# Attention with two dense stages on one core: the first keys on one queue, and other loads of the attention stage at other steps

## The chip, the cores and the metric

The kernel runs on one core of one Trainium2 chip. The metric is the device time of one execution in microseconds; the time before is the median of three executions, 612.26 us (610.55 to 615.47).

## The reference

The reference has three stages on one token matrix: an attention in which the 12 heads are mixed before and after the softmax, and two dense blocks.

```python
scores = scale * np.matmul(q, k.transpose(0, 1, 3, 2))       # batch 2, 12 heads, 448 x 448, head size 64
scores = np.einsum('bhij,hg->bgij', scores, w_pre)
scores = scores - np.max(scores, axis=-1, keepdims=True)
attn = np.exp(scores)
attn = attn / (np.sum(attn, axis=-1, keepdims=True) + 1e-09)
attn = np.einsum('bhij,hg->bgij', attn, w_post)
x = np.matmul(attn, v)                                       # then 896 tokens x 768
h = x @ moe_w_in;  x = np.where(h > 0, h, np.exp(np.minimum(h, 0)) - 1) @ moe_w_out
h = x @ moe2_w_in; x = (h / (1 + np.exp(-h))) @ moe2_w_out   # 768 -> 2048 -> 768, both times
```

All of it is in 32-bit floats.

## The kernel before, in words

The schedule is written out by hand: each engine executes its instructions in the order in which the program emits them, and each of the two load queues that are used (SP's and ACT's) issues its transfers in that order too.

**Start.** The queries come in seven tiles of 128 rows (`qT[T]`, all heads, 6 pairs of heads each), the keys as one tile per pair of heads (`kT[p]`, both batches side by side). Ahead of the loop the program issues, pair by pair, the keys of batch 0 (line 291), with the first query tile in two parts on ACT's queue (line 293); then the mixing weights `kpre` on ACT's queue, the second query tile, `kps`, a first part of v of batch 0 (heads 0 to 2, all partitions) and the third query tile on SP's queue. TensorE executes warm-up matmuls on zeros (line 306), then the scores of the first query tile, pair of heads by pair (`qk_pair`, line 148), in order of the pairs; ACT and DVE scale each pair's scores into `s` (lines 155 and 157).

**Blocks.** Mixing the heads needs the heads on the partitions. So 10 query rows of a tile make a block: a move from on-chip memory to on-chip memory (`move`, line 166) puts 10 rows of all 12 heads into the buffer `blk`, of which there are three, each for two blocks. `relayout(s)` issues the moves of step s, two to four of them, on SP's queue.

**Loop.** There are 45 steps. In step s TensorE executes `premix(s)` (line 196, reads `blk`), then attention times v for some heads of an older tile (`av_pair`, line 263, at the steps of `AV_AT`), then one pair of scores of a later query tile, then `postmix(s - 1)` (line 235). DVE takes the maximum, ACT the exponential, POOL scales the small weights `krn`, and ACT and DVE copy the result into `a`. At the end of step s the program issues `relayout(s + 2)` and then what the table `D_AT` holds for step s: query tiles, keys of batch 1 and parts of v, in this order, all on SP's queue. SP waits only where a buffer isn't free or a tile isn't there yet, so it is ahead of TensorE by some steps' worth of issues.

**Tables that bear on the change.** The keys of batch 1 are issued in steps 7 to 12, one pair in each. The fourth query tile (T = 3) is issued in step 7 and read in steps 10 to 15, one pair in each. v of batch 0 is loaded in parts of three heads (g) and half the partitions (u). `AV_AT` reads them so: step 8 reads heads 0 to 3, step 10 reads heads 4 to 7, step 12 reads heads 8 to 11; each matmul reads all partitions, so both halves u. In step 12 the matmuls on heads 8 and 9 alternate, so the second one already reads the part of heads 9 to 11 (g = 3). Before the change the parts g = 1 to 3 were issued in steps 2 to 7, one in each.

**Afterwards** come the two dense blocks, with each weight matrix split into a high and a low part (lines 497 to 549) and matmuls on both (lines 543, 805 and 1065). They are the larger part of the span.

Of the kernel before, what the change touches and what calls it, by code (L numbers as in the profile page):

```python
# [22 lines left out]
NP = H // 2  # L23
# [53 lines left out]
def attn_moe_moe(ctx: ExitStack, tc: tile.TileContext, q, k, v, w_pre, w_post, w1i, w1o, w2i, w2o, out):  # L77
    nc = tc.nc
# [34 lines left out]
    def load_q(T, eng=None, parts=(slice(0, NP),)):  # L113
        if T not in qT:
            qT[T] = wp.tile([P, NP, 2 * P], F32, name=f"qt{T}", tag="qT", bufs=3).rearrange("p a b -> p (a b)")[:, :NP * P].rearrange("p (a b) -> p a b", a=NP)
        for p in parts:
            (eng or nc.sync).dma_start(qT[T][:, p], q[T, :, p])

    def load_k(b, p, eng=None):
        if b == 0:  # L120
            kT[p] = kp.tile([P, 2, S], F32, name=f"kt{p}", tag=f"kT{p}")
        (eng or nc.sync).dma_start(kT[p][:, b], k[b, p])

    def load_v(b, u, g):

        h = slice(3 * g, 3 * g + 3)
        o = slice(0, P) if u is None else slice(HS * u, HS * u + HS)
        nc.sync.dma_start(vall[b][o, h].rearrange("p h r d -> p (h r d)"), v[b, o, 768 * g:768 * g + 768])
# [159 lines left out]
    nc.vector.memset(wz, 0.0)  # L288
    nc.vector.memset(pad[0:1], 0.0)
    for p in range(NP):  # L290
        load_k(0, p, (nc.sync, nc.scalar)[p in (2, 4)])
        if p < 2:
            load_q(0, nc.scalar, (slice(0, 2), slice(2, NP))[p:p + 1])
    nc.scalar.dma_start(kpre, w_pre)
# [25 lines left out]
    QK_AT, X_AT, D_AT = {}, {}, {}  # L320

    def at(d, step, f):
        d.setdefault(int(step), []).append(f)
# [2 lines left out]
        for p in range(LEAD if T == 1 else 0, NP):  # L326
            at(QK_AT, n0 + p, lambda T=T, p=p: qk_pair(T, p))
    for T in range(3, NQ):
        at(D_AT, (7, 13, 17, 24)[T - 3], lambda T=T: load_q(T))
    AV_AT = (8, 10, 12, 14, 16, 18, 20, 22, 23, 24, 26, 28, 30, 32, 34, 36, 38, 40, 42, 43, 44)  # L330
    for T in range(NT_ - 1):
        for p in range(NP):
# [3 lines left out]
    for g in range(4):  # L336
        for u in range(2):
            for b in range(B):
                if b == 1 or g > 0:
                    at(D_AT, 2 * g + u + (21 if b else 0), lambda b=b, u=u, g=g: load_v(b, u, g))  # L340

    def run(d, s):
        for f in d.get(s, []):
# [641 lines left out]
    x = [t[:, i] for t in rr for i in range(3)] + [xq[1, 5]] + [xq[1, p] for p in range(5)]  # L985
    xt[1] = {}
    for t, n_ in zip(x, "B11_0 B11_1 B11_2 T1_0 T1_1 T1_2 B21_0 B21_1 B22_0 T2_0 T2_1 B22_1 T3_0 T3_1 T4_0 T4_1 B21_2 T2_2 T3_2 T4_2 B22_2".split()):
        a, i = n_.split("_")
# [19 lines left out]
    for f in range(KF):  # L1008
        x = f + 2 if f < KS else f - KS
        raw[1, f] = rt[x // 3][:, x % 3] if x < 9 else rk[x - 9]  # L1010
    hb[1] = rk[3:]
    x = [ge[u][:, i] for u in range(2) for i in range(3)] + [gs[:, i] for i in range(6)]
# [106 lines left out]
    while n < NCH:  # L1119
# [5 lines left out]
        i = n - O2  # L1125
# [90 lines left out]
```

## Time and profile before

| | us |
|---|---|
| median of three runs | 612.26 |
| the three runs | 610.55, 612.26, 615.47 |
| the profiled execution | 608.93 |
| its span, first to last instruction | 607.1 |
| TensorE busy in it | 591.5 (97%) |
| VectorE, ScalarE, GpSimd busy | 451.0, 372.2, 62.7 |

The profile is of one execution, and its times are counted from the first instruction. An engine's busy time is the time in which it executes; a wait is time in which it is idle, and the profile says which event ended it. "SPq" and "ACTq" are the queues' issues of transfers: the time of such a row is that of issuing, not of moving the bytes. A transfer's landing is seen where somebody waits for it. The 45 steps of the attention stage lie in about the first quarter of the span.

### The profile page before, as it was taken

Reading aid. Unit: us, or ns where it says so; the run is one execution under the profiler, and the core shown is the slowest. Engines: PE = TensorE matmul, PEld = TensorE weight load, DVE = VectorE, ACT = ScalarE, POOL = GpSimd, SP = SyncE. Lnnn points to the kernel's source line nnn. Section 1 sums busy time; section 2 is a strip of 40 time slices with the busy share of each in tenths; the row PEclk is TensorE's granted clock in tenths of the full one; section 3 lists DMA queues with packets and bytes.
Section 4 is the critical chain, followed back from the end, with each engine's and each line's share of the span. In section 5 each row is a group of like instructions: output and inputs, shape, how many; then the busy total and the mean of one; then the engine's idle time right before and its main releaser. Section 6 shows DMA issues by size and latency. Waiting matters only on the chain.

```text
span 607.1 us, 14991 instructions
## 1 busy us (share of the span) xinstructions
PE 591.5 (97%) x6139; PEld 506.3 (83%) x6139; DVE 451.0 (74%) x756; ACT 372.2 (61%) x686; POOL 62.7 (10%) x117
## 2 busy tenths in 40 slices
PE   7899999998899999999999999999999999999997
PEld 2456766566699899999999999999999999999996
DVE  4777776888747999886776675599888888966642
ACT  4667776787838966758783553377676666533311
POOL 1222222247360000000000000000000000000000
PEclk9999999999999999999999999999999999999999
DMA  6577557755403243432434323434333323453601
GB/s 229 197 219 234 165 144 213 208 183 191 158 2 116 93 157 104 131 108 83 130 105 148 96 87 115 145 105 156 119 141 105 120 87 107 138 168 111 224 2 60
DMA packets 37682, 82.04 MB, mean 135 GB/s; under 512 B 4205, under 2 KB 18285, under 8 KB 37613
## 3 DMA queue, kind: packets, MB, share of 16 engines
q1 hardware_dynamic: 36749, 80.08, 41.7%
q8 instruction: 48, 0.79, 0.5%
q10 hardware_dynamic: 864, 1.00, 0.5%
q14 instruction: 21, 0.17, 0.1%
HBM read 59.05 MB, written 2.75 MB: 102 GB/s over the span
## 4 chain that ended last, share of the span: by engine, by line
PE 81%; DVE 6%; ACT 6%; DMA 5%; issue 1%; ACTq 0%; POOL 0%; DVEq 0%; SPq 0%; POOLq 0%
PE po L543 31%; PE b L805 28%; DMA blk<-s 4%; ACT pe L210 4%; PE av L263 4%; PE q L1065 4%; PE pre L196 3%; PE ph L529 3%; PE post L235 3%; PE pq L148 2%; PE po L1065 2%; DVE nmx L202 2%; DVE a L134 2%; PE post L529 1%; DMA kt<-in_k_dram 1%
## 5 line engine op out<-in xcount | busy, mean ns | idle before, releaser
L805 PE MATMUL b<-x,we 128*128 128x448 f32 x360 | 93.8, 363 | 0.0
L210 ACT ACTIVATE pe<-pre,nmx 124x448 f32<-124x448 f32 x90 | 56.3, 630 | 36.8 <-DVE nmx L202 35.9
L805 PEld LDWEIGHTS b<-x,we 128*128 128x128 f32 x360 | 67.5, 188 | 4.7 <-DVE we L549 0.2
L805 PE MATMUL b<-rr,we 128*128 128x448 f32 x288 | 69.5, 362 | 0.0
L757 ACT ACTIVATE wr<-wr 128x768 f32<-128x768 f32 (+1 forms) x61 | 52.9, 867 | 18.2 <-DMA wr<-in_w1o_dram 8.3
L235 PEld LDWEIGHTS post<-krn,pe 60*64 60x64 f32 x2520 | 45.6, 135 | 21.5 <-POOL krn L223 10.2
L543 PE MATMUL po<-ge,we 128*128 128x448 f32 x216 | 60.3, 362 | 0.0
L543 PE MATMUL po<-gs,we 128*128 128x448 f32 x216 | 59.9, 362 | 0.0
L753 DVE SCALAR_TENSOR_TENSOR wc<-wr,wc 128x768 int32<-128x768 int32 (+1 forms) x62 | 56.2, 907 | 3.9 <-ACT wr L757 0.4
L805 PEld LDWEIGHTS b<-rr,we 128*128 128x128 f32 x288 | 54.1, 188 | 3.5
L202 DVE TENSOR_REDUCE nmx<-pre 124x1 f32<-124x448 f32 x90 | 51.6, 615 | 4.2 <-PE pre L196 3.8
L196 PE MATMUL pre<-blk,kpre 64*64 64x448 f32 x360 | 48.7, 543 | 2.6 <-DMA blk<-s 2.0
L263 PEld LDWEIGHTS av<-a,v 128*64 128x64 f32 x768 | 36.9, 137 | 16.9 <-ACT pe L210 6.3
L543 PE MATMUL po<-x,we 128*128 128x448 f32 x192 | 50.1, 362 | 0.0
L235 PE MATMUL post<-krn,pe 60*64 60x60 f32 x2520 | 46.4, 219 | 3.6 <-POOL krn L223 2.8
L500 DVE TENSOR_TENSOR we<-wc,we 128x640 fp32r<-128x640 f32 (+1 forms) x31 | 26.7, 863 | 30.8 <-ACT we L491 30.8
L223 POOL TENSOR_SCALAR krn<-kps,sum 124x60 f32<-124x60 f32 x90 | 37.6, 432 | 113.3 <-DVE sum L219 96.4
L543 PE MATMUL po<-ta,we 128*128 128x448 f32 x168 | 44.8, 362 | 0.0
L148 PE MATMUL pq<-kt,qt 64*64 64x448 f32 x336 | 41.4, 561 | 2.5 <-ACT s L155 1.2
L263 PE MATMUL av<-a,v 128*64 128x120 f32 (+1 forms) x768 | 41.7, 262 | 1.6 <-ACT a L132 1.6
L543 PEld LDWEIGHTS po<-gs,we 128*128 128x128 f32 x216 | 40.6, 188 | 2.6
L543 PEld LDWEIGHTS po<-ge,we 128*128 128x128 f32 x216 | 40.6, 188 | 2.6
(155 smaller groups left out, 1079.4 us busy)
## 6 DMA issues: line engine op xcount, KB each, us to landing
blk<-s SPq DMA_DIRECT2D x77, 210.0 KB
wr<-in_w1i_dram SPq DMA_DIRECT2D x32, 384.0 KB
wr<-in_w2i_dram SPq DMA_DIRECT2D x32, 384.0 KB
wr<-in_w1o_dram SPq DMA_DIRECT2D x24, 384.0 KB
wr<-in_w2o_dram SPq DMA_DIRECT2D x24, 384.0 KB
wr<-in_w1o_dram SPq DMA_DIRECT2D x12, 256.0 KB
wr<-in_w2o_dram SPq DMA_DIRECT2D x12, 256.0 KB
v<-in_v_dram SPq DMA_DIRECT2D x14, 192.0 KB
```

The costliest lines, as they stand in the source:

```text
L148: nc.tensor.matmul(pq[e][HS * c:HS * c + HS], qT[T][half, p, HS * c:HS * c + HS], kT[p][half, bs[c % len(bs)]], start=True, stop=True, til ...
L196: nc.tensor.matmul(pre[s][r][HS * c:HS * c + HS], kpre[o], blkb[o, s % NBUF, c], start=True, stop=True, tile_position=(HS * r, HS * c))
L202: nc.vector.tensor_reduce(nmx[s][:n, r:r + 1], pre[s][r][:n], axis=AX.X, op=ALU.max, negate=True)
L210: nc.scalar.activation(t[:n], pre[s][r][:n], AF.Exp, bias=nmx[s][:n, r:r + 1], scale=1.0, accum_out=sums[s][:n, r:r + 1])
L223: nc.gpsimd.tensor_scalar(t[:n], kps[:n], z[:n, r:r + 1], None, op0=ALU.mult)
L235: nc.tensor.matmul(w[c][HS * u:HS * u + HS, r, j * BW:(j + 1) * BW], pexp[s][r][o, m * HS:(m + 1) * HS], kr[s][r][o].rearrange("p h i -> p ...
L263: nc.tensor.matmul(avt[T][e * D:(e + 1) * D, p % 2, :m], vall[b][:NV, h, j], amap[T][:NV, j * H + h, :m], start=j == 0, stop=j == 3, tile_ ...
L543: nc.tensor.matmul(po, wt[:, kk * P:(kk + 1) * P], g_op(moe, k0 + kk, hf, gi), start=(k0 == 0 and n_ == 0), stop=(k0 + kn == (KF, KS)[moe] ...
L753: nc.vector.scalar_tensor_tensor(cc, r[:, :, 1], 3, cc, op0=ALU.logical_shift_left, op1=ALU.bitwise_or)
L757: nc.scalar.activation(hf, hf, AF.Prelu, scale=2.0 ** -112, alpha=2.0 ** 32)
L805: nc.tensor.matmul(o, wt[:, u * KH + i * P:u * KH + (i + 1) * P], X[x, i][:, xi], start=start and n_ == 0, stop=n_ == 8, skip_group_check= ...
L1065: nc.tensor.matmul(o, wt[:, u * KH + i * P:u * KH + (i + 1) * P], t[i][:, xi] if x == "B22" else t[:, i, xi], start=start and n_ == 0, sto ...
```

## The change

Three things are changed. All six keys of batch 0 are issued on SP's queue, in the order of the pairs; before, pairs 2 and 4 were on ACT's queue. The fourth query tile is loaded in three parts of two pairs, in steps 7, 8 and 10, not whole in step 7. The parts of v of batch 0 (g, u) = (1,0), (1,1), (2,0), (2,1), (3,0), (3,1) are issued in steps 2, 4, 5, 6, 9, 11, not in steps 2 to 7. The parts of v of batch 1 stay in steps 21 to 28.

```diff
     for p in range(NP):
-        load_k(0, p, (nc.sync, nc.scalar)[p in (2, 4)])
+        load_k(0, p)
         if p < 2:
             load_q(0, nc.scalar, (slice(0, 2), slice(2, NP))[p:p + 1])
...
     for T in range(3, NQ):
-        at(D_AT, (7, 13, 17, 24)[T - 3], lambda T=T: load_q(T))
+        for i, s in enumerate(((7, 8, 10), (13,), (17,), (24,))[T - 3]):
+            at(D_AT, s, lambda T=T, x=slice(2 * i, 2 * i + 2) if T == 3 else slice(0, NP): load_q(T, None, (x,)))
...
                 if b == 1 or g > 0:
-                    at(D_AT, 2 * g + u + (21 if b else 0), lambda b=b, u=u, g=g: load_v(b, u, g))
+                    at(D_AT, 2 * g + u + 21 if b else (2, 4, 5, 6, 9, 11)[2 * g + u - 2], lambda b=b, u=u, g=g: load_v(b, u, g))
```

## Rows read from the trace of the kernel before

**Rows 1.** The page, its chain that ended last, by engine.

```profile
PE 81%; DVE 6%; ACT 6%; DMA 5%; issue 1%; ACTq 0%; POOL 0%; DVEq 0%; SPq 0%; POOLq 0%
```

**Rows 2.** Stretches: bounds, length, busy by engine (instructions), clock, DMA share, GB/s.

```profile
2.00:4.00 2.00, 1.98 (x4) 0.67 (x2) 0.09 (x1) 0.00 (x0) 1.05 (x1) 1.00 0.89 315
4.00:6.00 2.00, 1.98 (x12) 0.74 (x16) 0.11 (x1) 1.62 (x3) 0.00 (x0) 1.00 1.05 349
6.00:8.00 2.00, 0.84 (x12) 0.24 (x8) 1.14 (x2) 0.94 (x2) 0.00 (x0) 1.00 1.01 379
...
36.00:42.00 6.00, 5.67 (x110) 3.34 (x112) 4.42 (x11) 4.24 (x12) 1.67 (x4) 1.00 0.86 227
...
48.00:54.00 6.00, 6.00 (x176) 4.23 (x174) 4.41 (x9) 3.80 (x10) 0.84 (x2) 1.00 0.76 227
```

**Rows 3.** Timeline of the start: start, duration, engine, line, operation, [idle before].

```profile
0.73 0.89 ACTq L117 DMA_DIRECT2D qt<-in_q_dram  x2
0.73 1.81 SPq L122 DMA_DIRECT2D kt<-in_k_dram  x4
...
1.38 2.60 PE L306 MATMUL warm<-wz 128*128 128x448 f32 x4 [1.38 <-DVE align L289]
...
1.65 0.93 ACTq L122 DMA_DIRECT2D kt<-in_k_dram  x2
...
4.02 2.54 PE L148 MATMUL pq<-kt,qt 64*64 64x448 f32 x16
...
7.72 5.73 PE L148 MATMUL pq<-kt,qt 64*64 64x448 f32 x56 [1.16 <-DMA kt<-in_k_dram]
```

**Rows 4.** Chain of waits up to 70 us: start, duration, what.

```profile
1.65 5.93 DMA kt<-in_k_dram
...
11.75 2.83 DMA blk<-s
...
33.42 5.59 DMA blk<-s
...
40.53 6.35 DMA blk<-s
```

**Rows 5.** Timeline of SP's queue, steps 7 to 11.

```profile
36.60 1.64 SPq L117 DMA_DIRECT2D qt<-in_q_dram  x1
38.29 0.42 SPq L122 DMA_DIRECT2D kt<-in_k_dram  x1
38.75 0.75 SPq L128 DMA_DIRECT2D v<-in_v_dram  x1
39.61 1.71 SPq L166 DMA_DIRECT2D blk<-s  x2
...
48.79 1.71 SPq L166 DMA_DIRECT2D blk<-s  x2
50.54 0.51 SPq L122 DMA_DIRECT2D kt<-in_k_dram  x1
```

**Rows 6.** Timeline of TensorE, steps 10 to 13.

```profile
45.76 0.97 PE L196 MATMUL pre<-blk,kpre 64*64 64x448 f32 x4
46.92 0.97 PE L196 MATMUL pre<-blk,kpre 64*64 64x448 f32 x4 [0.20 <-DMA blk<-s]
...
53.55 0.94 PE L196 MATMUL pre<-blk,kpre 64*64 64x448 f32 x8
54.42 1.86 PE L263 MATMUL av<-a,v 128*64 128x120 f32 x32
```

**Rows 7.** The page, DMA issues: what, queue, operation, count, KB each.

```profile
v<-in_v_dram SPq DMA_DIRECT2D x14, 192.0 KB
```

**Rows 8.** DMA issues of the whole span, the same columns.

```profile
qt<-in_q_dram SPq DMA_DIRECT2D x6, 384.0 KB
kt<-in_k_dram SPq DMA_DIRECT2D x10, 224.0 KB
```

**Rows 9.** Waits of TensorE, whole span: total us, times, longest us.

```profile
PE pre L196 <- DMA blk<-s: 2.0, 4, 1.3
```

## The prediction

> **What bounds the kernel now.** I read the chain of waits first. 81% of it is TensorE, 5% is transfers [rows 1], and the dense blocks, which the change doesn't touch, hold most of the TensorE part. So only a few microseconds can move. Next I looked in the attention stage for the places where the chain passes through a transfer. Four pieces bear on the change [rows 4]. The first is the keys, 5.93 us from an issue at 1.65 to a landing at 7.58. The second is the first block move, 2.83 us. The last two are moves of steps 6 and 8, 5.59 and 6.35 us. The block moves have the same kind and size, so the reader sees a queue: with little ahead of it a move lands 2.83 us after its issue, and from about 33 us on two to three times as late. The stretches agree, with 0.86 and 0.76 of the transfer engines busy at 227 GB/s in the last two lines of [rows 2]. Third, the timeline of TensorE: the second half of the mixing of step 10 starts at 46.92 after a start of the first at 45.76 [rows 6], when its move has landed at 40.53 + 6.35 = 46.88 [rows 4].
>
> My sum is made against the profiled execution, 608.93 us with a span of 607.1. The median of the runs shown is 612.26, so 3.33 us more; I add the sum to the median.
>
> **First keys.** TensorE finishes the scores of pairs 0 and 1 at 4.02 + 2.54 = 6.56 and starts pair 2 at 7.72; 1.16 us of idle time are put down to keys [rows 3]. These are the keys of pair 2, third on ACT's queue behind two parts of the queries, while SP's queue moves pairs 3 and 5, which are wanted later. The transfer engines are full meanwhile (share 0.89 to 1.05), with 315, 349 and 379 GB/s in three stretches [rows 2], so the bytes ahead decide. In the new order pair 2 needs 384 + 3 x 224 = 1056 KB [rows 8], 1081 thousand bytes. By 4.00 us 630 thousand have moved, and the other 451 take 1.29 us at 349 GB/s: 5.29. Pair 0 gives the lag to the use: its 128 + 224 KB, 360 thousand bytes, are moved by 2 + 360/315 = 3.14, and it starts at 4.02, 0.88 later. So pair 2 is there at 6.17, before TensorE is through with pair 1. The pairs behind need 229 thousand bytes each, 0.6 to 0.66 us at these rates, and are used one per 5.73/7 = 0.82 us [rows 3], so no new wait follows. On SP the two issues that join the queue cost 2 x 0.45 us (1.81 for four [rows 3]); they lie beside the transfers, which are late anyway. The next issue on SP, the second query tile, moves behind them by at most 0.9 us, and its scores come after those of pair 5. Two issues leave ACT's queue, where nothing waits for them. Bounds: between nothing (the slowest transfer engine, not the mean, sets a landing) and 1.16 us. I take a gain of 1.0, nearer to the row of the wait. All of it lies on the path: the scores of pair 5 release the first move at 11.75 [rows 4].
>
> The Trainium skill, in "DMA: Bandwidth & Descriptors", section "Issuing engines are not separate DMA queues", says that transfers issued by different engines run on the same 16 engines and that issuing from several saves issue time alone. By that rule alone the edit would gain nothing and lose up to those 0.9 us, and the sum below would be 3.2 in place of 1.3. The rule leaves out that of the bytes on their way some are wanted earlier than others.
>
> **Fourth query tile and v.** In step 7 SP issues q (384 KB), keys (224) and v (192) ahead of the moves at 39.61 [rows 5, 7, 8]. After the change it issues 128 + 224 KB there. 448 KB less stand ahead of the moves for step 10, about 459/227 = 2.0 us of transfer, so the 1.16 us between the halves of the mixing in step 10 [rows 6] should go. The parts of the queries in steps 8 and 10 add two issues of about 0.4 us (the keys' 0.42 [rows 5]) on SP, which is ahead of TensorE. Parts one to three are read from steps 10, 12 and 14 on, at least two steps behind their issue; I cost them at nothing, and the cover is those two steps, 7.8 us as from 45.76 to 53.55 [rows 6], against a landing in 5.59 to 6.35.
>
> What is late next is v. From step 7 to step 11 SP issues 384 + 5 x 224 + 192 = 1696 KB before, and 1888 KB after, for the v part of step 3 drops out early, where it disturbed nobody, and two parts come late. So at step 11 the queue isn't shorter but 192 KB longer. The last part, (3,1), is issued at the end of step 11, behind the moves at 48.79 and the keys, which are issued at 50.54 + 0.51 = 51.05 [rows 5]. TensorE starts the attention times v of step 12 at 54.42 [rows 6] and its second matmul needs this part. **The price:** with the landing times of the loaded queue, 5.59 and 6.35, the part lands at 56.6 to 57.4; with that of the empty one, 2.83, at 53.9. The stretch from 48 to 54 moves 227 GB/s, as that from 36 to 42 [rows 2], so the loaded rows are the nearest. Against 54.42 that is 2.2 to 3.0 us late, and nothing in the other bound. I take 2.3, near the low end, since SP reaches the place a little earlier when step 7 gives it less to issue. Behind the waiting matmul stand all later TensorE instructions: the scores, the mixing after the softmax of step 11 and the mixing of step 13, and with them the maxima on DVE and the exponentials on ACT. From 48 to 54 TensorE is busy for 6.00 of 6.00 us [rows 2], so it can't catch up. The 1.16 us of step 10 aren't subtracted from this: TensorE only comes earlier to the place where it waits for the landing, and its idle time there grows to about 3.4 us.
>
> The wait of the moves that land at 39.01 (33.42 + 5.59) stays, since the v parts of steps 4 to 6, which stand around them, stay.
>
> **Sum:** -1.0 + 2.3 = +1.3 us. 608.93 becomes 610.2, the median 613.6.
>
> **Rivals.**
> *The part lands in time.* The queue would have to be drained by step 11; the moves land 2.83 us behind their issue where it is [rows 4], and the bound of 53.9 lies before 54.42. Against it stand the two loaded rows. Then both gains hold: -1.0 - 1.16 = -2.2, a median of 610.1.
>
> *The clock falls in the stall, which makes the kernel slower by more.* The first 16 score matmuls take 2.54 us, 0.159 each, and the later 56 take 5.73, 0.102 each [rows 3]: until then TensorE had executed nothing but the warm-up from 1.38 on, and it runs slower, though the granted clock is given as 1.00 in these stretches [rows 2]. Its longest waits for transfers are 1.3 us [rows 9] and don't show this afterwards (the 56 follow one of 1.16). A stall of 3.4 us is longer than any of these. From that length on, if the clock then falls to the lower of its two levels, 1.2 GHz, the price is between 16 x 0.057 = 0.9 us and half of the 5.2 us from 1.38 to 6.56, that is 2.6; I take 2.0. Sum +3.3, a median of 615.6. "TensorE: Matmul & The Clock Gate" of the Trainium skill, section "HAM oscillation — how this bites in real kernels", describes such a fall in waits for transfers; no row here shows a wait as long as this stall.
>
> *The first keys gain nothing,* as the change in order may not do what it says if the slowest transfer engine is late with pair 2 in any order: and the two issues on SP then cost up to 0.9 us: +2.3 to +3.2, a median of 614.6 to 615.5. For it speaks that shares above 0.89 hide single engines; against it the order of the bytes.
>
> **How the numbers follow.** Chances: the forecast 0.58, the part in time 0.22, the clock 0.13, no gain from the keys 0.07. The likeliest gives 613.6. Its own bounds are -1.16 + 2.2 to +3.0 (a key gain of nothing), so 613.3 to 615.3. The three runs of before lie between -1.7 and +3.2 of their median, so a median of such runs can be off by 1 to 2. The range takes in the rival below with that, 609, and the one above, 617. A change of 1%, 6.1 us, is about what a measurement of this kernel can tell from none. For the faster side all gains that I find make 2.2; for the slower side the highest price is 3.0 + 2.6 = 5.6. So faster 0.02, same 0.94, slower 0.04.
>
> **What would show it.** Right: pair 2 starts without a wait for keys, near 6.6, and the first move is issued near 10.8; the halves of step 10's mixing are no longer apart; in step 12 TensorE idles for some 3 us within the first matmuls on v, put down to the landing of v, and the mixing of step 13 starts 1 to 2 us later than before. Wrong: the matmuls on v in step 12 follow the mixing at once (then it is -2.2), or those behind the stall take twice their time (+3.3). The forecast also fails if a later stage gives the time back, which would show as a shorter span behind the attention stage.

## The result, and the profile after

The changed kernel takes 615.55 us (median of 22 runs), the kernel before in the same runs 611.87 us. The ratio is 1.0076 (95% interval 1.0055 to 1.0097), some 4.6 us of 612. Each ratio in this document comes from the single runs, without the executions in a slower state that some kernels have (up to 627 us), so it isn't the quotient of the two medians, which here differ by 3.7 us. The profiled execution of the changed kernel takes 615.15 us with a span of 613.3, so 6.2 us over that of before.

The chain of waits of the changed kernel, up to 75 us (start, duration, what), answers to [rows 4]:

```profile
3.98 7.41 PE pq L148 x56
11.39 2.83 DMA blk<-s
...
32.25 6.38 DMA blk<-s
...
44.99 1.34 issue
...
51.82 5.68 DMA v<-in_v_dram
...
57.63 2.15 PE av L263 x30
```

The keys are gone from it, and the first block move is issued at 11.39, not 11.75. The move of step 6 is as late as before (32.25 + 6.38 = 38.63, before 39.01). Two new pieces have come: 1.34 us in which TensorE waits for nothing that the profile names ("issue"), and a load of v that lands at 57.50.

TensorE's timeline of the changed kernel (start, duration, line, operation, [idle before]), which answers to [rows 3, 6]:

```profile
3.97 9.12 PE L148 MATMUL pq<-kt,qt 64*64 64x448 f32 x72
...
44.48 0.51 PE L235 MATMUL post<-krn,pe 60*64 60x60 f32 x18
46.33 0.74 PE L235 MATMUL post<-krn,pe 60*64 60x60 f32 x35 [1.34 <-issue]
...
53.54 0.94 PE L196 MATMUL pre<-blk,kpre 64*64 64x448 f32 x8
54.41 0.42 PE L263 MATMUL av<-a,v 128*64 128x120 f32 x2
57.63 2.15 PE L263 MATMUL av<-a,v 128*64 128x120 f32 x30 [2.80 <-DMA v<-in_v_dram]
59.71 1.77 PE L148 MATMUL pq<-kt,qt 64*64 64x448 f32 x8
61.26 1.51 PE L235 MATMUL post<-krn,pe 60*64 60x60 f32 x56
62.60 0.93 PE L196 MATMUL pre<-blk,kpre 64*64 64x448 f32 x8
```

The last of these rows, the mixing of step 13, is in the kernel before

```profile
57.83 0.94 PE L196 MATMUL pre<-blk,kpre 64*64 64x448 f32 x8
```

Up to the first matmul on v in step 12 nothing is won or lost: 54.41 against 54.42. One matmul later the wait for v begins, and the mixing of step 13 starts at 62.60, 4.77 us late. Of this, 3.1 are the delay from 54.42 to the landing at 57.50 (TensorE itself is idle for 2.80). The rest comes behind it: the scores take 1.77 us where they take 0.98 otherwise, and the mixing after the softmax 1.51 in place of 0.99. The stretches of the changed kernel show why (bounds, length, busy by engine, granted clock, DMA share, GB/s):

```profile
56.00:59.00 3.00, 1.37 (x27) 1.40 (x29) 0.74 (x3) 1.33 (x4) 0.83 (x2) 1.00 0.79 225
59.00:62.00 3.00, 3.00 (x44) 1.70 (x44) 0.37 (x1) 0.77 (x2) 0.00 (x0) 0.50 0.84 231
62.00:65.00 3.00, 3.00 (x114) 2.07 (x112) 2.33 (x5) 1.42 (x5) 0.00 (x0) 0.93 0.07 21
```

The granted clock is 0.50 from 59 to 62, the level of 1.2 GHz, after the stall of 2.80 us. SP's queue of the changed kernel, steps 7 and 11, answers to [rows 5]:

```profile
35.41 0.50 SPq L117 DMA_DIRECT2D qt<-in_q_dram  x1
35.95 0.47 SPq L122 DMA_DIRECT2D kt<-in_k_dram  x1
36.52 1.87 SPq L166 DMA_DIRECT2D blk<-s  x2
...
51.30 0.48 SPq L122 DMA_DIRECT2D kt<-in_k_dram  x1
51.82 1.66 SPq L128 DMA_DIRECT2D v<-in_v_dram  x1
```

The moves for step 10, which SP issues in step 8 right behind the loads of step 7, are issued 3 us earlier than before, at 36.52 for 39.61. The last v part is issued at 51.82 and lands 5.68 us later.

### The profile page after: what moved, and what is told of

Its sections match the earlier page's. It is cut to its first block, busy times and chain, and to the rows that moved or that the text cites. A ratio compares the mean times of both kernels' runs of the same rounds, so it can differ in the third digit from the quotient of the medians.

```text
span 613.3 us, 14995 instructions
## 1 busy us (share of the span) xinstructions
PE 593.5 (97%) x6139; PEld 507.1 (83%) x6139; DVE 451.4 (74%) x756; ACT 372.4 (61%) x686; POOL 62.7 (10%) x117
## 4 chain that ended last, share of the span: by engine, by line
PE 82%; ACT 6%; DVE 6%; DMA 4%; issue 1%; SPq 0%; DVEq 0%; ACTq 0%
PE po L544 31%; PE b L806 28%; PE av L263 4%; ACT pe L210 4%; PE q L1066 4%; PE pq L148 3%; PE ph L530 3%; DMA blk<-s 3%; PE pre L196 3%; PE post L235 3%; PE po L1066 2%; DVE nmx L202 2%; DVE a L134 2%; PE post L530 1%; DMA v<-in_v_dram 1%
## 5 line engine op out<-in xcount | busy, mean ns | idle before, releaser
L196 PE MATMUL pre<-blk,kpre 64*64 64x448 f32 x360 | 47.4, 542 | 2.4 <-DMA blk<-s 2.0
L148 PE MATMUL pq<-kt,qt 64*64 64x448 f32 x336 | 42.9, 585 | 1.3 <-ACT s L155 1.2
```

What stands on the lines that cost most here:

```text
L148: nc.tensor.matmul(pq[e][HS * c:HS * c + HS], qT[T][half, p, HS * c:HS * c + HS], kT[p][half, bs[c % len(bs)]], start=True, stop=True, til ...
L196: nc.tensor.matmul(pre[s][r][HS * c:HS * c + HS], kpre[o], blkb[o, s % NBUF, c], start=True, stop=True, tile_position=(HS * r, HS * c))
```

## Experiments

Theory: the v part of step 11 stands behind a loaded queue, lands late, and the stall lowers the clock. The keys in order gain a little. The rivals are given with each run. All times are against runs of the kernel before on the same chip. Where a heading says "only", the kernel before is edited, else the changed kernel.

**Only the v parts moved.**

```diff
-at(D_AT, 2 * g + u + (21 if b else 0), ...
+at(D_AT, 2 * g + u + 21 if b else (2, 4, 5, 6, 9, 11)[2 * g + u - 2], ...
```

> The kernel before with the v parts of batch 0 in steps 2 to 11 and nothing else changed. Theory (the last v part lands late for step 12, and the stall lowers the clock): TensorE waits 2.5 to 4 us for v in step 12, as 2.80 us in the changed kernel, and a stretch of about 3.4 us at half the granted clock follows; 3 to 6 us slower than before. Rival (the loss comes from waits of TensorE's own instruction issue, 1.34 us in step 10 of the changed kernel, and the stall at v is made good later): within 1.5 us of before.

Measured: 615.59 us, ratio 1.0072 (1.0046 to 1.0099), as much as the whole change loses. TensorE's timeline of this kernel:

```profile
54.08 0.42 PE L263 MATMUL av<-a,v 128*64 128x120 f32 x2
58.17 3.46 PE L263 MATMUL av<-a,v 128*64 128x120 f32 x30 [3.68 <-DMA v<-in_v_dram]
61.56 0.98 PE L148 MATMUL pq<-kt,qt 64*64 64x448 f32 x8
...
63.18 0.94 PE L196 MATMUL pre<-blk,kpre 64*64 64x448 f32 x8
```

A stall of 3.68 us, and then 30 rows on v that take 3.46 us, where 32 take 1.86 at the higher level [rows 6]. Its granted clock from 58 to 61.5 is 0.52. The theory holds. The chain of waits has the load itself, issued at 51.25 and landed at 58.13:

```profile
51.25 6.88 DMA v<-in_v_dram
```

**Only the keys on one queue.**

```diff
-        load_k(0, p, (nc.sync, nc.scalar)[p in (2, 4)])
+        load_k(0, p)
```

> The kernel before with all first keys on SP's queue and nothing else changed. Theory: the wait of 1.16 us for keys goes, and the first block move is issued 0.3 to 1.1 us before 11.75; 0.3 to 1.1 us faster. Rival (the start is set by when the clock rises, 5.70 us in the profile before and 7.79 in the one after, and not by the keys): between 0.3 us faster and 1 us slower, the more the later the clock rises in its profile.

Measured: 610.24 us, ratio 0.9983 (0.9956 to 1.0010): a gain of 1.0 us, the size that the theory gives, but the interval contains 1, so it isn't shown. In its chain the wait for keys is gone and the first move is issued at 10.64, 1.1 us earlier than before:

```profile
3.98 6.66 PE pq L148 x56
10.64 2.83 DMA blk<-s
```

The changed kernel has the same start and its move at 11.39. The difference is in the speed of the same 56 rows, 7.41 against 6.66 us. The first score matmuls up to 8 us (ns, least/median/most) are, in the kernel before and in the changed one:

```profile
L148 PE MATMUL pq<-kt,qt x20: 537/599/1006, 4.0 to 7.7; 64*64 64x448 f32 x20
```

```profile
L148 PE MATMUL pq<-kt,qt x24: 547/951/1005, 4.0 to 7.8; 64*64 64x448 f32 x24
```

TensorE starts slow, at some 1,000 ns, and in this execution of the changed kernel stays so for longer: the median is 951 ns, not 599. So part of what the keys give is decided by when the speed rises, which differs from execution to execution.

The kernel with only the v parts moved shows how much: it has the old order of the keys, and TensorE doesn't wait for them in its profile either. The first row is its timeline, the second its chain of waits:

```profile
4.09 8.64 PE L148 MATMUL pq<-kt,qt 64*64 64x448 f32 x72
```

```profile
11.03 2.83 DMA blk<-s
```

Its first move is issued at 11.03, before the 11.39 of the changed kernel. In the three profiles with the old order it is issued at 11.03, 11.21 and 11.75, in the ten with the new order between 10.22 and 11.39. So the two orders overlap: the wait of 1.16 us isn't there in every execution of the old order, and 1.16 us isn't what each execution gains.

The profiled execution with only the keys moved lost its lead late in the attention stage, in waits for issue that the kernel before doesn't have in this place (TensorE's timeline):

```profile
103.73 0.85 PE L235 MATMUL post<-krn,pe 60*64 60x60 f32 x43 [1.22 <-issue]
...
110.58 1.30 PE L263 MATMUL av<-a,v 128*64 128x88 f32 x29 [2.49 <-issue]
```

**The changed kernel with the v parts back in steps 2 to 7.**

```diff
-at(D_AT, 2 * g + u + 21 if b else (2, 4, 5, 6, 9, 11)[2 * g + u - 2], ...
+at(D_AT, 2 * g + u + (21 if b else 0), ...
```

> The changed kernel with the v parts back in steps 2 to 7: the first keys on one queue and the query tile in three parts stay. Theory: no wait for v, no fall of the clock; 0.3 to 2.2 us faster than before. Rival (the issue waits and the fuller queue of the three parts make the loss): 1 to 3 us slower than before, with a wait for issue of about 1.3 us near step 10.

Measured: 611.17 us, ratio 0.9975 (0.9938 to 1.0012), no wait for v and no fall of the clock. The loss is gone; a gain of 1.5 us fits the theory and isn't shown. The rival's wait is there too, though: between 36 and 60 us TensorE waits as follows (total, times, longest).

```profile
PE post L235 <- issue: 2.0, 2, 1.2
```

So the other two parts of the change aren't where the loss is: together they cost 0.7 us at most, the end of the interval. In this execution 2.0 us of waits for issue stand against what they give; what these cost in the mean isn't shown.

**Only the query tile in three parts.**

```diff
-        at(D_AT, (7, 13, 17, 24)[T - 3], lambda T=T: load_q(T))
+        for i, s in enumerate(((7, 8, 10), (13,), (17,), (24,))[T - 3]):
+            at(D_AT, s, lambda T=T, x=slice(2 * i, 2 * i + 2) if T == 3 else slice(0, NP): load_q(T, None, (x,)))
```

> The kernel before with the fourth query tile in three parts and nothing else changed. Theory (256 KB less ahead of the moves of step 10): the second half of step 10's mixing waits 0 to 0.6 us in place of about 1.0, no wait for v; 0 to 1 us faster. Rival (the two extra issues cost as much as they spare, or the spared wait comes back as a wait for issue): within 0.5 us either way, with a wait for issue of over 1 us that the kernel before doesn't have there.

Measured: ratio 1.0001 (0.9970 to 1.0033), 0.0 us. The mixing of step 10 still takes longer than its 0.94:

```profile
43.98 1.48 PE L196 MATMUL pre<-blk,kpre 64*64 64x448 f32 x8
```

Before, its halves lay 1.16 us apart [rows 6] and the whole took 2.13; over half of the delay is spared in this execution. It doesn't show in the ratio. The rival's wait for issue isn't in this profile, but by the times theory and rival aren't told apart.

**Extra matmuls in the stall.** The changed kernel with 48 matmuls on v's first part ahead of those that wait.

```diff
+        for x in range(48 if (T, p) == (0, 4) else 0):
+            e = x % 2
+            nc.tensor.matmul(avt[T][e * D:(e + 1) * D, 0, :m], vall[b][:NV, e, 0], amap[T][:NV, e, :m], start=True, stop=True, tile_position=(0, e * D))
```

> The changed kernel with 48 extra matmuls on v's first part (2.8 us, their output is written over) ahead of the attention times v of step 12, so that TensorE is busy while the last v part is on its way. Theory: v lands at the same time, 57 to 58 us, and the granted clock stays high, so step 13 starts 1 to 1.7 us earlier than in the changed kernel; 2.5 to 3.5 us slower than before. Rival (the stretch at half the clock has another cause than the idle time): as slow as the changed kernel, about 4.6 us over before, with the stretch at half the clock still there.

Measured: 617.89 us, ratio 1.0093 (1.0056 to 1.0131). The forecast of the time missed. The place itself does what the theory says, though the fill takes 5.14 us, not 2.8 (each matmul is two rows):

```profile
52.91 5.14 PE L262 MATMUL av<-a,v 128*64 128x120 f32 x96
57.88 1.81 PE L266 MATMUL av<-a,v 128*64 128x120 f32 x32
...
61.23 0.94 PE L196 MATMUL pre<-blk,kpre 64*64 64x448 f32 x8
```

Behind the fill 32 rows take 1.81 us, at the higher level. In the profile another wait for issue stands in the same stage, of 3.1 us and ending at 111.14, with a granted clock of 0.63 in the 3 us from 111 on; whether this makes the other runs long isn't shown (TensorE's waits up to 160 us):

```profile
PE post L235 <- issue: 3.7, 2, 3.1
```

So a second try had few instructions: 6 score matmuls.

```diff
+        if (T, p) == (0, 4):
+            fl = ps.tile([P, S], F32, name="fill", tag="av", bufs=1)
+            for x in range(6):
+                e, c = 0, x % 2
+                nc.tensor.matmul(fl[HS * c:HS * c + HS], qT[2][e * D:(e + 1) * D, 0, HS * c:HS * c + HS], kT[0][e * D:(e + 1) * D, 0], start=True, stop=True, tile_position=(e * D, HS * c))
```

> The changed kernel with 6 extra score matmuls (some 2.3 us, their output is thrown away) ahead of the attention times v of step 12: TensorE is busy through most of the stall, with few instructions more, where the fill of 48 had 96 rows more and took longer than the stall. Theory: v lands as late as in the changed kernel and the granted clock stays high behind it; 2 to 3.5 us slower than before. Rival (the clock has little to do with the loss in the mean over many runs): 4 us or more slower than before, as the changed kernel and the fill of 48.

Measured: 614.77 us, ratio 1.0059 (1.0024 to 1.0094), 3.6 us over before, just outside the forecast. TensorE's timeline:

```profile
53.20 2.48 PE L261 MATMUL fill<-kt,qt 64*64 64x448 f32 x12
55.74 0.42 PE L268 MATMUL av<-a,v 128*64 128x120 f32 x2
56.70 1.82 PE L268 MATMUL av<-a,v 128*64 128x120 f32 x30 [0.54 <-DMA v<-in_v_dram]
...
60.08 0.94 PE L196 MATMUL pre<-blk,kpre 64*64 64x448 f32 x8
```

Its stretch behind the fill, with the granted clock at 1.00:

```profile
56.00:59.00 3.00, 2.46 (x40) 1.95 (x42) 0.34 (x2) 0.63 (x3) 0.83 (x2) 1.00 0.85 254
```

From where the matmuls on v go on to the mixing of step 13 it is 60.08 - 56.70 = 3.38 us here and 61.23 - 57.88 = 3.35 with the fill of 48, but 62.60 - 57.63 = 4.97 in the changed kernel and 5.01 with only the v parts moved. In both kernels in which TensorE is busy in the meantime the clock doesn't fall, and the fall costs 1.6 us. That is shown in the place, by one profile of each kernel. The intervals of the ratios 1.0059 and 1.0076 overlap, so it isn't shown over the runs.

**The last v part one step earlier.**

```diff
-(2, 4, 5, 6, 9, 11)[2 * g + u - 2]
+(2, 4, 5, 6, 9, 10)[2 * g + u - 2]
```

> The changed kernel with the last v part issued in step 10 and not in step 11; all else as changed. Theory: two moves and one pair of keys (2.0 + 0.8 us in the changed kernel) no longer stand ahead of it, so it lands 2.5 to 3 us earlier; TensorE waits 0 to 0.9 us for v in step 12, the granted clock stays high; 1 us faster to 1.5 us slower than before, 3 to 5 us faster than the changed kernel. Rival (v is late through the fuller queue as a whole): a wait for v of over 2 us, 3 us or more slower than before.

Measured: 611.85 us, ratio 1.0004 (0.9977 to 1.0032), and TensorE waits for v not at all. One load moved by one step takes back 0.72% of 612 us, 4.4 us, which is about the stall and the fall of the clock in the profile, 3.1 + 1.6. With the kernel in which only the v parts moved, this settles the place of the loss. The profile by itself wouldn't: TensorE reaches the matmuls on v of step 12 only at 56.74, 2.3 us later than before, behind a wait for issue of 3.20 us

```profile
51.79 0.68 PE L235 MATMUL post<-krn,pe 60*64 60x60 f32 x13 [3.20 <-issue]
52.16 0.96 PE L196 MATMUL pre<-blk,kpre 64*64 64x448 f32 x1
```

with a granted clock of 0.50 right behind it:

```profile
52.00:53.00 1.00, 1.00 (x20) 0.60 (x20) 0.43 (x1) 0.47 (x1) 0.00 (x0) 0.50 0.65 183
```

So the clock also fell behind a wait that isn't one for a transfer of data.

**The last two parts in steps 8 and 9.**

```diff
-(2, 4, 5, 6, 9, 11)[2 * g + u - 2]
+(2, 4, 5, 6, 8, 9)[2 * g + u - 2]
```

> The changed kernel with the two last v parts issued in steps 8 and 9, not 9 and 11. Theory: no wait for v, no fall of the clock; the gains of the first keys and of step 10 hold, 0.5 to 2 us faster than before. Rival (the late parts only move the wait to the block moves of steps 10 to 12): a wait for a move of 1 us or more in steps 11 or 12, within 0.5 us of before or slower.

Measured: 610.70 us, ratio 0.9980 (0.9950 to 1.0011). TensorE reaches the matmuls on v of step 12 at 53.36, earlier than before, and doesn't wait for v. But the mixing of step 12 now takes 2.18 us and is released by a move, so the rival has its part; the time fits the theory, but its interval contains 1:

```profile
51.25 2.18 PE L196 MATMUL pre<-blk,kpre 64*64 64x448 f32 x8 [0.25 <-DMA blk<-s]
53.36 1.86 PE L263 MATMUL av<-a,v 128*64 128x120 f32 x32
```

**Parts spread over steps 2 to 9, none in step 5.**

```diff
-(2, 4, 5, 6, 9, 11)[2 * g + u - 2]
+(2, 3, 4, 6, 8, 9)[2 * g + u - 2]
```

> The changed kernel with the v parts in steps 2, 3, 4, 6, 8, 9, so that no part is issued in step 5. Theory: one part less stands ahead of the moves of step 8, so the second half of its mixing waits about 0.5 us less; 1 to 2.5 us faster than before, the fastest of all. Rival (waits for issue and chance at later steps outweigh it): no faster than the kernel with the parts in 8 and 9, within 1 us of before.

Measured: 609.81 us, ratio 0.9958 (0.9928 to 0.9988), 2.6 us faster than before, just over the forecast; from the kernel with parts in 8 and 9 it isn't told apart, as the intervals overlap. In steps 8 and 10 both halves of the mixing run side by side, without a wait:

```profile
36.96 0.94 PE L196 MATMUL pre<-blk,kpre 64*64 64x448 f32 x8
...
43.55 0.94 PE L196 MATMUL pre<-blk,kpre 64*64 64x448 f32 x8
```

That step 5 is the reason isn't shown: the changed kernel with v back in steps 2 to 7 has a part in step 5, and its profile has the mixing of step 8 side by side too:

```profile
36.44 0.94 PE L196 MATMUL pre<-blk,kpre 64*64 64x448 f32 x8
```

The profiled execution of the spread kernel, 613.41 us, isn't one of its faster ones; it has waits of 1.84 and 2.21 us for issue at 105 and 111 us. A second job had the same kernel again, with no edit.

> The kernel with the v parts of batch 0 in steps 2, 3, 4, 6, 8, 9, unchanged, in a second job. Theory: 1 to 4.5 us faster than before, as 0.9958 (0.9928 to 0.9988) in the first. Rival (the first job's verdict was chance): within 1 us of before.

Measured: 609.33 us, ratio 0.9962 (0.9936 to 0.9988). The gain holds. Its profile also shows a price: the mixing of step 12 takes 2.97 us in place of 0.94 (some 1.3 in the first profile):

```profile
50.81 2.97 PE L196 MATMUL pre<-blk,kpre 64*64 64x448 f32 x8
```

**And the parts of batch 1 seven steps earlier.**

```diff
-at(D_AT, 2 * g + u + 21 if b else (2, 3, 4, 6, 8, 9)[2 * g + u - 2], ...
+at(D_AT, 2 * g + u + 14 if b else (2, 3, 4, 6, 8, 9)[2 * g + u - 2], ...
```

> The kernel with the v parts of batch 0 in steps 2, 3, 4, 6, 8, 9, and in addition those of batch 1 in steps 14 to 21, not 21 to 28 (they are first read in step 30). Theory (a full queue of transfers costs waits for moves and for issue near 105 to 117 us): these waits shrink; 1 us or more faster than the kernel without this, 3 to 6 us faster than before. Rival (the queue is as full in steps 14 to 21, so the waits only move): within 1 us of the kernel without this.

Measured: 607.85 us, ratio 0.9949 (0.9926 to 0.9971), 3.1 us faster than before and the fastest of all. Against the kernel without this in the same job it is 1.5 us by the medians, with overlapping intervals. The waits for issue near 105 to 117 us are gone from its profile, but others have come, in the steps to which the loads were moved:

```profile
74.26 1.45 PE L263 MATMUL av<-a,v 128*64 128x120 f32 x23 [1.36 <-issue]
...
81.61 1.08 PE L235 MATMUL post<-krn,pe 60*64 60x60 f32 x32 [2.31 <-issue]
```

That the waits for issue go with the loads would fit: in both profiles of the spread kernel they end at the same two places (105.08 and 111.69; 105.56 and 112.17). But the kernel before and the one with parts in 8 and 9 load v of batch 1 in the same steps and have none there, so the loads alone don't make them, and the cause isn't shown. The page of the profile lists transfers of kind "instruction" beside the data's; that these come late when many transfers are on their way is a guess that no run here tests.

## Why the prediction came out as it did

The measured time lies in the range and within 1% of before, but near the upper end. The mechanism of the forecast, a late v part that TensorE waits for, was right; its price was too low, and a fall of the clock belonged to it.

- **What bounds the kernel.** Right: the loss is in the attention stage, and the larger part of it is a wait for a transfer. Near the end of that stage, where TensorE goes on behind a wait for POOL at 154.08 us for 148.08, the changed kernel's execution is 6.00 of its 6.2 us behind.
- **First keys, a gain of 1.0.** The wait of 1.16 us went, as forecast. What arrived at the first move was 0.36 us in the changed kernel's profile and 1.1 with the keys alone, as TensorE's slow first stretch ended later in the one than in the other. The step at fault is that the whole wait was counted as a gain, from one execution; with the old order and a late rise of the speed there is no such wait. In the ratio the keys alone give 1.0 us, with an interval that contains 1. That no new wait follows was right in the changed kernel's profile; in that of the kernel with parts in 8 and 9 TensorE waits 0.36 us for the keys of pair 3.
- **The wait in step 10.** That its 1.16 us go and still don't count was right, for more reasons than given: in the changed kernel a wait for issue of 1.34 us took their place ahead of the stall.
- **The price of the late v part, 2.3.** Issue 51.82 (forecast 51.05), landing 5.68 us later (5.59 to 6.35), at 57.50 (56.6 to 57.4). The delay from 54.42 is 3.1, the upper bound and not the 2.3 taken near the lower. The reason for the low end failed: SP had less to issue in step 7, and was indeed ahead there by 3 us, but by step 11 it issued this part 0.8 us later than forecast. The two further query parts stand in between, but they explain at most 0.6 us: with only the v parts moved, and so without them, it is issued at 51.25 and lands 6.88 us later, above the upper bound. By the chain of waits the move ahead of it was released by TensorE in both kernels (at 50.71 and 49.99), so what SP gained in step 7 didn't last to step 11.
- **The clock.** This was a rival with 0.13, and the sum left it out. It came true in both kernels in which TensorE waits for v with nothing put in between. Its price was put at 2.0 and is 1.6. The prediction's own sign for it, matmuls behind the stall that take twice their time, was there in the scores (1.77 for 0.98). With it the forecast gave 615.6 and the median is 615.55, but that this agrees so well is luck: in the place the terms are nothing for the keys, 3.1 for the delay and 1.6 for the clock, 4.7 in sum and not 3.3, and the median of before in the same runs is 611.87, not 612.26. The step that was wrong is the choice against the fall: the prediction named an idle time of 3.4 us, longer than any in the trace of before, and then took the higher level for granted. The section that the prediction cites from the Trainium skill ("TensorE: Matmul & The Clock Gate", section "HAM oscillation — how this bites in real kernels") describes such a fall in waits for transfers. The trace agrees, with a granted clock of 0.50 from 59 to 62 us.
- **The move that lands at 39.01.** Right, 38.63 in the changed kernel. The reason given, the v parts of steps 4 to 6, isn't borne out: in two other kernels with a part in step 5 (v back in steps 2 to 7, and the last part in step 10) the mixing of step 8 takes 0.94 without a gap.
- **The profiled execution** is 6.2 us longer in span, of which 4.77 are there by step 13. A wait for issue of 1.20 us at 121 us, which the profile of before doesn't have, is most of the rest; the ratio over the runs gives 4.6.

## What to carry to other kernels

Price a load that is moved late by the landing time of the queue at that place, not by that of an empty queue, and count all bytes that still stand ahead of it: a later issue of the same bytes doesn't make the queue shorter at the last one. If the sum says that TensorE will idle for longer than anywhere in the trace, add the fall of its clock to the sum rather than to the list of rivals. When a load has to move, leave it more than one step to its reader (here step 11 for step 12 lost 4.6 us, step 10 lost nothing that is shown), and look at what it then delays: with parts in 8 and 9 the moves of step 12 came late. And don't take a wait seen in one execution at its full length for the gain: the start of this kernel differs by over 1 us from execution to execution.

## What the runs showed of the hardware that was not expected

- TensorE's granted clock fell to 0.50 behind waits of 2.80, 3.10, 3.20 and 3.68 us, and behind shorter ones of 2.21 (both profiles of the spread kernel) and 2.31 (with the parts of batch 1 moved too). It didn't behind 2.19 (with 6 extra matmuls) and 2.49 (only the keys moved). What decides between these is open.
- TensorE waited for issue for 1.2 to 3.2 us in the attention stage, in nine of the thirteen profiles, at places that differ from kernel to kernel; in the kernel before the only such wait is of 0.7 us. These waits are as large as the gains of the later versions, and their cause is open.
- The speed of the first score matmuls rose at different times in different executions, which moved the issue of the first block move between 10.22 us (with 6 extra matmuls) and 11.39 (the changed kernel) at the same order of the first keys.
